# A product that begins half a row of retention earlier, and weight tiles that are converted later

## The chip, the cores and the metric

The kernel runs on one core of a Trainium2 chip. The metric is device time in microseconds for one launch. The version before took 604.58 us, the median of three runs (603.8, 604.58 and 605.14).

## The reference

Two stages follow each other. The first is a linear attention with decay (retention) over 4 batches, 8 heads, 768 tokens and a head width of 64:

```
state = gamma * state + k_t v_t^T
y_t   = scale * q_t state
```

Its output, laid out as 3072 tokens by 512 features, is x of a feed-forward layer with 2048 inner features:

```
h = x @ w_in                      # 3072x512 by 512x2048
g = h * clip(h + 3, 0, 6) / 6
out = g @ w_out                   # 3072x2048 by 2048x512
```

q, k and v are float32. Both weight matrices are float64 and are turned into float32 on the chip.

## The kernel before, in words

**Retention.** The 3072 tokens are 24 *rows* of 128 tokens. For a row, TensorE forms all scores of the eight heads (`sc`, L253, 16 matmuls), VectorE masks them (`am`, L301), TensorE forms the row's output from the state before it (`y`, L239, 8 matmuls) and from the masked scores (`y`, L259, 8 matmuls), and adds the row's keys and values to the running state (`uz`, L288, 8 matmuls), which ScalarE copies out (`state`, L297). VectorE scales the output (`xr`, L274), ScalarE writes its rounded high part and VectorE the remainder (`x`, L133 and L134). `burst(r)` does the scores of row r together with the output of row r-1; `sc` and `y` have one PSUM buffer each, so the scores of one row wait for the mask of the row before, and the output of one row for `xr` of the row before. The values are weighted per head by ScalarE for the first eight rows (`early`, L212, eight small instructions a row) and by GpSimd afterwards (L216).

**First product.** Four rows are a *unit* of 512 tokens, six units in all. `mm1(u, jj)` makes one 128x512 tile of h for unit u and feature tile jj (of 16): 12 matmuls, four blocks of the 512 features by three pairs of high and low parts. ScalarE adds 3 and takes the relu (L358), VectorE clips and multiplies (`g`, L359), and the tile goes out to a DRAM buffer (`gd`, L360). Three PSUM tiles and three SBUF tiles serve h and g.

**Weights of w_in.** Each of the 16 tiles of w_in is fetched as 512 KB of float64 (`st`, L104, two buffers, so the third fetch waits until the first has been converted) and converted by five VectorE instructions with one of ScalarE between them (L115 to L127), and then split into a high part (ScalarE, L133) and a low part (VectorE, L134). `build_w1(j)` is tile j. Tiles of w_out are converted in the same way (`build_w2`) during later units, with four more subtractions.

**Second product.** When all six units are through, `out` is made from `gd` by a seven-product scheme (L401 to L471). Nothing of it is touched here.

**Order.** TensorE's order is written by hand, in the order in which the program calls `burst` and `mm1`. VectorE, ScalarE, GpSimd and the transfer queue of SyncE are put in order by a scheduler when the program is built; on the chip each of them works its list off in that order. At the start `load` and `load_decay` of rows 0 to 7 are issued on SyncE, with four fetches of w_in between them (`WITH`, L51), and no transfer is issued before the one eight places ahead of it has landed. `attention` is a generator with one stop per row, `advance(n)` runs it up to its n-th stop, and the list `steps` (L366 to L369) says in which order the products are called: four of unit 0, then one of unit 0 and one of unit 1 in turn, then the other units.

Of the kernel before, what the change touches and what calls it, by code (L numbers as in the profile page):

```python
# [29 lines left out]
def retention_ffn(ctx: ExitStack, tc: tile.TileContext, qkv, w_in, w_out, dvs, dqs, out, B, H, S, D):  # L30
# [8 lines left out]
    NF = w_in.shape[0]  # L39
# [3 lines left out]
    NROW = NT // P  # L43
    ROWS_B = S // P
    UR = 4
# [2 lines left out]
    HM = DM // 2  # L48
    WARM = 14
    AHEAD = 2 * UR  # L50
    WITH = (0, 2, 3, 5)  # L51
    BUFS = {"lkt": 1, "lqt": 2, "lvn": 2, "lkn": 1}
    SPARE = ("lkn", "lkt", "lqt", "lqt")
    BLK = 2 * P
# [47 lines left out]
    def fetch(src):  # L102
        st = wst.tile([P, src.shape[-1]], I64, tag="st", name=nm("st"), bufs=2)
        nc.sync.dma_start(out=st, in_=src)  # L104
        return st
# [26 lines left out]
    def split(hi, lo, src):  # L132
        nc.scalar.activation(out=hi, in_=src, func=AF.Copy)  # L133
        nc.vector.tensor_tensor(out=lo, in0=src, in1=hi, op=ALU.subtract)  # L134
# [8 lines left out]
    def w1_block(j, k):  # L143
        s, o = divmod(j * NK + k, 14)
        if s not in w1s:
            w1s[s] = place([P, 14, 2, P], F32R, nm("w1"), s == 0)
        return w1s[s], o

    def build_w1(j, st=None):
        w = to_f32(fetch(w_in[j]) if st is None else st).rearrange("p (k n) -> p k n", k=NK)  # L150
        k = 0
        while k < NK:
            t, o = w1_block(j, k)
            n = min(NK - k, 14 - o)
            split(t[:, o : o + n, 0], t[:, o : o + n, 1], w[:, k : k + n])
            k += n
# [31 lines left out]
    def load(r):  # L188

        t = rows[r] = {}
        if r < AHEAD and r % 2 == 0:
            early[r] = wpool.tile([P, 7, NPAIR, P], F32, tag="w", name=nm("early"), bufs=NSLOT - 1)
        for i, (x, n) in enumerate((("kt", 1), ("qt", 0), ("vn", 3), ("kn", 2))):
            o = r % 2 * 4 + i
            if r < AHEAD and o < 7:
                t[x] = early[r // 2 * 2][:, o]
            else:  # L200
                tag = SPARE[r // 2] if r < AHEAD else f"l{x}"
                t[x] = apool.tile([P, NPAIR, P], F32, tag=tag, name=nm(x), bufs=BUFS[tag])
            if x != "kn" or r % ROWS_B < ROWS_B - 1:
                nc.sync.dma_start(out=t[x].rearrange("p h n -> p (h n)"), in_=qkv[r, n])
        if r >= AHEAD:
            decay(r)
# [13 lines left out]
    def load_decay(r):  # L220
        if r < AHEAD:
            if "dq" not in early:
                early["dq"] = wpool.tile([P, ROWS_B, NPAIR, P], F32, tag="w", name=nm("early"), bufs=NSLOT - 1)
            t = early["dq"][:, r % ROWS_B]
        else:
            t = apool.tile([P, NPAIR, P], F32, tag="dq", name=nm("dq"), bufs=1)
        rows[r]["dq"] = t
        if r < ROWS_B or r >= AHEAD:
            nc.sync.dma_start(out=t.rearrange("p h n -> p (h n)"), in_=dqs[r % ROWS_B])
# [82 lines left out]
    def attention():  # L312

        st = []
        for r in range(AHEAD):
            load(r)
            load_decay(r)
            if r in WITH:
                st.append(fetch(w_in[len(st)]))
        decay(0)  # L320
        for r in range(NROW + 1):
            if r == AHEAD:
                burst(r, new=False)
                yield
                burst(r, old=False)
            else:
                burst(r)
            if st and r in (0, 2, 3, 4):
                build_w1(len(WITH) - len(st), st.pop(0))
            if r + 1 < AHEAD:  # L330
                decay(r + 1)
            if r >= AHEAD - 1 and r + 1 < NROW:
                load(r + 1)
            if AHEAD <= r < NROW:
                load_decay(r)
            yield

    gen = attention()
    done = 0

    def advance(n):

        nonlocal done
        while done < min(n, NROW + 2):
            next(gen)
            done += 1

# [15 lines left out]
    order = ExitStack()  # L363
    order.enter_context(tc.manual_schedule(engines={mybir.EngineType.PE}))

    steps = [(0, jj) for jj in range(UR)]  # L366
    for jj in range(NF):
        steps += [(0, jj + UR)] * (jj + UR < NF) + [(1, jj)]
    steps += [(u, jj) for u in range(2, NU) for jj in range(NF)]  # L369
    advance(UR + 1)  # L370
    n_w1, n_w2 = len(WITH), 0
    for n, (u, jj) in enumerate(steps):
        if (u, jj) == (NU - 1, 0):
            att.close()
            late = ctx.enter_context(tc.tile_pool(name="late", bufs=1, side="right", reuse_waits="tile"))
        while n_w1 < min(NF, jj + 4):
            build_w1(n_w1)
            n_w1 += 1
        if jj in WHEN.get(u, ()):
            build_w2(n_w2)  # L380
            n_w2 += 1
        end = mm1(u, jj)
        if n < UR:
            advance(UR + 2 + n)
        elif u == 1:
            advance(2 * UR + 2 + int((jj + 1) / NF * UR + 0.5))
        elif 1 < u < NU - 1:
            advance(UR * (u + 1) + 2 + int((jj + 1) / NF * UR + 0.5))
    order.close()
    ph1.close()  # L390

# [146 lines left out]
```

## Time and profile before

| what | value |
|---|---|
| median of three runs | 604.58 us |
| the profiled execution's own time | 606.66 us |
| its span, first to last instruction | 604.9 us |
| TensorE (PE) busy | 588.3 us, 97% of the span |
| VectorE (DVE) busy | 457.4 us, 76% |
| ScalarE (ACT) busy | 253.1 us, 42% |
| GpSimd (POOL) busy | 18.0 us, 3% |
| mean granted clock of TensorE | 0.991 |

A page of the profile shows one execution. The share of busy time is a mean over stages with different limits, and a TensorE that runs at half its clock counts as busy. So the stretches of the first 140 us are read one by one: which engine has idle time in them, what ended it, and which clock was granted.

### The profile page before, as it was taken

To read this page: it belongs to the slowest core of one execution; us is meant where nothing else is said; L and a number is where in the kernel's file an instruction comes from. 1 tells how busy PE (TensorE), PEld (TensorE's weight loads), DVE (VectorE), ACT (ScalarE), POOL (GpSimd) and SP (SyncE) were. 2 spreads that over 40 slices of the span, in tenths; PEclk is the share of its full clock that TensorE was granted. 3 is DMA by queue.
4 is the path that set the end of the run, shared out by engine and by line. 5 is a ranking of instruction groups with operands and counts; after the bars stand their busy time and mean duration, and the time that the engine had idled before them with its cause. 6 is when DMAs were issued, how large, how long until landed. Compare 5 with 4: busy or idle time off the path is not lost.

```text
span 604.9 us, 12611 instructions
## 1 busy us (share of the span) xinstructions
PE 588.3 (97%) x4988; PEld 524.5 (87%) x4988; DVE 457.4 (76%) x960; ACT 253.1 (42%) x540; POOL 18.0 (3%) x24
## 2 busy tenths in 40 slices
PE   7688999999999999999999999999999999999997
PEld 6567788777888888888888889999999999999997
DVE  4779999999433597334336969998899889988983
ACT  5663554445222343222225545444444444444441
POOL 0001000000100000000000000000000000000000
PEclk9879999999999999999999999999999999999999
DMA  8965777665754457444334435443444344434411
GB/s 325 390 226 172 226 260 246 207 235 185 257 170 166 163 206 265 151 173 172 136 125 153 159 117 178 140 141 105 140 140 141 105 140 140 142 113 135 143 64 36
DMA packets 64731, 104.13 MB, mean 172 GB/s; under 512 B 5792, under 2 KB 30880, under 8 KB 64672
## 3 DMA queue, kind: packets, MB, share of 16 engines
q1 hardware_dynamic: 64528, 103.31, 50.7%
q8 instruction: 39, 0.64, 0.5%
q14 instruction: 20, 0.16, 0.1%
q10 hardware_dynamic: 144, 0.02, 0.0%
HBM read 71.85 MB, written 31.46 MB: 171 GB/s over the span
## 4 chain that ended last, share of the span: by engine, by line
PE 78%; DVE 14%; DMA 3%; issue 2%; SPq 1%; ACT 0%; DVEq 0%; ACTq 0%
PE o L440 40%; PE h L354 32%; PE y L259 3%; PE sc L253 2%; DVE g L359 2%; DMA st<-in_w_in 2%; DVE wb L121 2%; DVE w L134 2%; DVE am L301 2%; DVE we L124 2%; DVE ww L127 1%; PE y L239 1%; DMA early<-in_qkv 1%; DVE xr L274 1%; DVE ws L86 1%
## 5 line engine op out<-in xcount | busy, mean ns | idle before, releaser
L354 PE MATMUL h<-x,w 128*128 128x512 f32 x1152 | 272.4, 395 | 4.2 <-ACT x L133 2.2
L354 PEld LDWEIGHTS h<-x,w 128*128 128x128 f32 x1152 | 215.5, 189 | 53.6 <-DVE g L359 2.8
L440 PEld LDWEIGHTS o<-w,gc 128*128 128x128 f32 x2016 | 239.9, 191 | 0.1
L440 PE MATMUL o<-w,gc 128*128 128x256 f32 x2016 | 239.9, 282 | 0.0
L359 DVE SCALAR_TENSOR_TENSOR g<-g,h 128x512 f32<-128x512 f32 x96 | 65.7, 685 | 86.0 <-ACT g L358 85.7
L358 ACT ACTIVATE g<-h,three 128x512 f32<-128x512 f32 x96 | 65.5, 684 | 100.0 <-PE h L354 92.9
L133 ACT ACTIVATE gc<-gr 128x256 fp32r<-128x256 f32 x144 | 49.6, 408 | 117.8 <-PE o L440 114.1
L134 DVE TENSOR_TENSOR gc<-gr,gc 128x256 fp32r<-128x256 f32 x144 | 52.7, 420 | 20.1 <-ACT gc L133 20.1
L134 DVE TENSOR_TENSOR gc<-gsum,gc 128x768 fp32r<-128x768 f32 x96 | 62.0, 687 | 5.6 <-ACT gc L133 5.6
L133 ACT ACTIVATE gc<-gsum 128x768 fp32r<-128x768 f32 x96 | 54.7, 618 | 0.1
L133 ACT ACTIVATE w<-ww 128x384 fp32r<-128x384 f32 (+2 forms) x34 | 18.8, 556 | 50.9 <-DVE ww L127 48.4
L301 DVE TENSOR_TENSOR am<-sc,mask 128x1024 f32<-128x1024 f32 x24 | 29.2, 1216 | 0.0
L119 ACT ACTIVATE we<-we,ebias 128x512 int32<-128x512 int32 x32 | 22.9, 715 | 11.7 <-DVE we L115 11.5
L216 POOL TENSOR_TENSOR vn<-vn,cst_sb 128x512 f32<-128x512 f32 x16 | 17.2, 1078 | 272.0 <-DMA vn<-in_qkv 272.0
L124 DVE SCALAR_TENSOR_TENSOR we<-st,we 128x512 int32<-128x512 int32 x32 | 22.7, 711 | 0.0
L134 DVE TENSOR_TENSOR w<-ww,w 128x384 fp32r<-128x384 f32 (+2 forms) x34 | 20.3, 601 | 3.1 <-ACT w L133 2.9
L127 DVE SCALAR_TENSOR_TENSOR ww<-wb,we 128x512 f32<-128x512 f32 x32 | 22.1, 690 | 0.7
L121 DVE SCALAR_TENSOR_TENSOR wb<-st,wb 128x512 f32<-128x512 uint32 x32 | 22.0, 686 | 0.2
L89 DVE TENSOR_TENSOR gsum<-gr 128x256 f32<-128x256 f32 x48 | 20.4, 425 | 2.0 <-DMA gr<-gd 0.6
L133 ACT ACTIVATE x<-xr 128x512 fp32r<-128x512 f32 x24 | 15.1, 629 | 14.3 <-DVE xr L274 14.3
L86 DVE TENSOR_TENSOR gsum<-gr,gsum 128x256 f32<-128x256 f32 x48 | 20.2, 421 | 0.8
L115 DVE TENSOR_SCALAR we<-st 128x512 int32<-128x512 int32 x32 | 13.5, 422 | 9.2 <-DMA st<-in_w_in 8.9
(50 smaller groups left out, 349.8 us busy)
## 6 DMA issues: line engine op xcount, KB each, us to landing
gd<-g SPq DMA_DIRECT2D x96, 256.0 KB, 2.5
gr<-gd SPq DMA_DIRECT2D x96, 256.0 KB, 3.2
st<-in_w_in SPq DMA_DIRECT2D x16, 512.0 KB, 4.3
st<-in_w_out SPq DMA_DIRECT2D x16, 512.0 KB, 3.9
early<-in_qkv SPq DMA_DIRECT2D x28, 256.0 KB, 6.0
out<-ot SPq DMA_DIRECT2D x11, 512.0 KB, 2.8
kn<-in_qkv SPq DMA_DIRECT2D x16, 256.0 KB, 4.4
kt<-in_qkv SPq DMA_DIRECT2D x16, 256.0 KB, 3.9
```

Of the source, the lines that this page charges most:

```text
L86: return nc.vector.tensor_tensor(out=out_, in0=a, in1=b, op=ALU.subtract)
L119: nc.scalar.activation(out=e, in_=e, func=AF.Relu, scale=8.0, bias=ebias)
L121: nc.vector.scalar_tensor_tensor(out=y, in0=lo.bitcast(U32), scalar=2.0**-32, in1=b, op0=ALU.mult, op1=ALU.add)
L124: nc.vector.scalar_tensor_tensor(out=e, in0=hi, scalar=-2147483648, in1=e, op0=ALU.bitwise_and, op1=ALU.bitwise_or)
L127: nc.vector.scalar_tensor_tensor(out=w, in0=y, scalar=2.0**-20, in1=e.bitcast(F32), op0=ALU.mult, op1=ALU.mult)
L133: nc.scalar.activation(out=hi, in_=src, func=AF.Copy)
L134: nc.vector.tensor_tensor(out=lo, in0=src, in1=hi, op=ALU.subtract)
L301: nc.vector.tensor_tensor(out=new["am"].rearrange("p h a n -> p (h a) n"), in0=sc.rearrange("p h a n -> p (h a) n"), in1=mask[:, None, :]. ...
L354: nc.tensor.matmul(h, t[:, o, a], xs[u][b][:, k], start=k + n == 0, stop=(k, n) == (NK - 1, 2), skip_group_check=True)
L358: nc.scalar.activation(out=g, in_=h, func=AF.Relu, bias=three)
L359: ins = nc.vector.scalar_tensor_tensor(out=g, in0=g, scalar=6.0, in1=h, op0=ALU.min, op1=ALU.mult)
L440: nc.tensor.matmul(ps, gc[:, a, LEFT[i], jj, :], wc[:, RIGHT[i], b_], start=first and j == 0 and n == 0, stop=j == NFP - 1 and n == 2, ski ...
```

## The change

Five things are altered, all at the start of the program:

- The four early fetches of w_in stand behind rows 0, 3, 4 and 6 of the loads instead of rows 0, 2, 3 and 5.
- The burst of row 4 is cut in two, as that of row 8 was before: first the output of row 3, then a stop, then the scores of row 4.
- Tiles 1, 2 and 3 of w_in are converted behind the first half of row 4, behind its second half and behind row 5, instead of behind rows 2, 3 and 4.
- The number of products of unit 0 ahead of the first one of unit 1 goes from five to six (`LEAD`), and the rows that come one behind each product are rows 4 (second half) to 8 (first half).
- The counts given to `advance` are one higher, since there is one stop more.

```diff
-    WITH = (0, 2, 3, 5)
+    WITH = (0, 3, 4, 6)
+    LEAD = UR + 1
...
-            if r == AHEAD:
+            if r in (UR, AHEAD):
                 burst(r, new=False)
+                if r == UR:
+                    build_w1(1, st[1])
                 yield
                 burst(r, old=False)
             else:
                 burst(r)
-            if st and r in (0, 2, 3, 4):
-                build_w1(len(WITH) - len(st), st.pop(0))
+            if r == 0:
+                build_w1(0, st[0])
+            elif r in (UR, UR + 1):
+                build_w1(r - 2, st[r - 2])
...
-        while done < min(n, NROW + 2):
+        while done < min(n, NROW + 3):
...
-    steps = [(0, jj) for jj in range(UR)]
+    steps = [(0, jj) for jj in range(LEAD)]
     for jj in range(NF):
-        steps += [(0, jj + UR)] * (jj + UR < NF) + [(1, jj)]
+        steps += [(0, jj + LEAD)] * (jj + LEAD < NF) + [(1, jj)]
...
-        if n < UR:
+        if n < LEAD:
             advance(UR + 2 + n)
         elif u == 1:
-            advance(2 * UR + 2 + int((jj + 1) / NF * UR + 0.5))
+            advance(2 * UR + 3 + int((jj + 1) / NF * UR + 0.5))
         elif 1 < u < NU - 1:
-            advance(UR * (u + 1) + 2 + int((jj + 1) / NF * UR + 0.5))
+            advance(UR * (u + 1) + 3 + int((jj + 1) / NF * UR + 0.5))
```

How the engines' lists move is shown at three places. The names carry a number that tells buffers apart; the lines of the changed kernel are one to five higher.

TensorE around the first four products, before (`h_493`, `h_572`, `h_660` and `h_741` are the products of unit 0 with tiles 0 to 3; each `sc` is the scores of a row, from row 4 on):

```order
L253 MATMUL sc_430<-early_152 64x128 x16
L259 MATMUL y_421<-am_400,early_136 64x128 x8
L288 MATMUL uz<-early_152 64x64 x8
L354 MATMUL h_493<-x_258,w_19_221 128x512 x12
L239 MATMUL y_510<-early_152,state_398 64x128 x8
L253 MATMUL sc_519<-early_152 64x128 x16
L259 MATMUL y_510<-am_469,early_152 64x128 x8
L354 MATMUL h_572<-x_258,w_19_221 128x512 x12
```

And in the changed kernel (`h_431` and `h_510` are the products with tiles 0 and 1):

```order
L240 MATMUL y_399<-early_136,state_329 64x128 x8
L260 MATMUL y_399<-am_389,early_136 64x128 x8
L359 MATMUL h_431<-x_258,w_19_221 128x512 x12
L254 MATMUL sc_448<-early_150 64x128 x16
L289 MATMUL uz<-early_150 64x64 x8
L359 MATMUL h_510<-x_258,w_19_221 128x512 x12
L240 MATMUL y_527<-early_150,state_387 64x128 x8
L254 MATMUL sc_536<-early_150 64x128 x16
```

The scores and the state of row 4 have moved from ahead of the first product to behind it, and the second product comes ahead of the output of row 4.

VectorE from the second row on, before (`xr_317` is the output of row 1, `we_334` the second tile of w_in):

```order
L134 TENSOR_TENSOR x_258<-xr_259,x_258 128x4x128
L115 TENSOR_SCALAR we_334<-st_142 128x512
L116 TENSOR_SCALAR wb_333<-st_142 128x512
L121 SCALAR_TENSOR_TENSOR wb_333<-st_142,wb_333 128x512
L274 TENSOR_TENSOR xr_317<-y_283,early_126 128x512
L301 TENSOR_TENSOR am_331<-sc_292,mask 128x1024
```

And in the changed kernel (`xr_317` and `xr_375` are the outputs of rows 1 and 2, `we_421` the second tile of w_in):

```order
L135 TENSOR_TENSOR x_258<-xr_259,x_258 128x4x128
L275 TENSOR_TENSOR xr_317<-y_283,early_126 128x512
L302 TENSOR_TENSOR am_331<-sc_292,mask 128x1024
L135 TENSOR_TENSOR x_258<-xr_317,x_258 128x4x128
L116 TENSOR_SCALAR we_421<-st_148 128x512
L117 TENSOR_SCALAR wb_420<-st_148 128x512
L122 SCALAR_TENSOR_TENSOR wb_420<-st_148,wb_420 128x512
L125 SCALAR_TENSOR_TENSOR we_421<-st_148,we_421 128x512
L275 TENSOR_TENSOR xr_375<-y_341,early_126 128x512
```

The first instruction of the second tile stood ahead of the output of row 1 and stands now ahead of the output of row 2.

VectorE around the first products' results, before (`g_506` and `g_585` are the results of the first two products, `ww_473` the fourth tile of w_in, `we_562` the fifth):

```order
L127 SCALAR_TENSOR_TENSOR ww_473<-wb_471,we_472 128x512
L134 TENSOR_TENSOR w_19_221<-ww_473,w_19_221 128x2x128
L134 TENSOR_TENSOR w_50_482<-ww_473,w_50_482 128x2x128
L359 SCALAR_TENSOR_TENSOR g_506<-g_506,h_493 128x512
L274 TENSOR_TENSOR xr_545<-y_510,early_126 128x512
L301 TENSOR_TENSOR am_549<-sc_519,mask 128x1024
L134 TENSOR_TENSOR x_544<-xr_545,x_544 128x4x128
L115 TENSOR_SCALAR we_562<-st_559 128x512
```

And in the changed kernel (`g_444` and `g_523` are the first two results, `ww_479` the third tile of w_in, `we_499` the fifth; the fourth, `we_569` from `st_168`, stands nine rows after `we_499`):

```order
L128 SCALAR_TENSOR_TENSOR ww_479<-wb_477,we_478 128x512
L135 TENSOR_TENSOR w_19_221<-ww_479,w_19_221 128x4x128
L364 SCALAR_TENSOR_TENSOR g_444<-g_444,h_431 128x512
L302 TENSOR_TENSOR am_475<-sc_448,mask 128x1024
L364 SCALAR_TENSOR_TENSOR g_523<-g_523,h_510 128x512
L116 TENSOR_SCALAR we_499<-st_496 128x512
L117 TENSOR_SCALAR wb_498<-st_496 128x512
L275 TENSOR_TENSOR xr_562<-y_527,early_126 128x512
```

Before, four tiles of w_in are converted ahead of the first result; now three are, both first results stand ahead of the fifth tile, and the fourth tile is converted behind the fifth.

## Rows read from the trace of the kernel before

**Rows 1.** Busy time of each engine by stretch: from and to in us, the stretch's length, then for PE, PEld, DVE, ACT and POOL busy us and instructions, then the granted clock of TensorE (1.00 is 2.4 GHz, 0.50 is 1.2 GHz), the DMA share and GB/s.

```profile
17.50:21.00 3.50, 0.76 (x20) 0.52 (x24) 3.34 (x6) 2.24 (x6) 0.00 (x0) 1.00 1.06 398
21.00:24.50 3.50, 3.50 (x50) 3.17 (x52) 2.86 (x5) 2.54 (x8) 0.00 (x0) 0.51 1.04 383
...
29.00:31.00 2.00, 0.17 (x6) 0.03 (x2) 1.91 (x4) 1.58 (x5) 0.00 (x0) 1.00 1.06 389
31.00:38.00 7.00, 6.13 (x20) 4.10 (x24) 4.93 (x9) 4.25 (x15) 0.00 (x0) 0.52 0.49 186
38.00:49.00 11.00, 11.00 (x168) 9.01 (x160) 9.18 (x15) 6.80 (x20) 1.24 (x1) 1.00 0.76 253
49.00:50.50 1.50, 0.49 (x10) 0.30 (x13) 1.50 (x2) 1.21 (x2) 0.00 (x0) 1.00 0.68 251
...
62.50:100.00 37.50, 37.50 (x334) 30.81 (x334) 37.12 (x67) 18.28 (x32) 1.04 (x1) 1.00 0.72 241
100.00:130.00 30.00, 29.94 (x192) 23.86 (x189) 29.76 (x64) 13.96 (x24) 1.05 (x1) 1.00 0.67 225
130.00:140.00 10.00, 9.17 (x40) 6.90 (x39) 9.94 (x18) 4.46 (x8) 1.06 (x1) 1.00 0.53 177
140.00:200.00 60.00, 60.00 (x536) 49.43 (x538) 29.08 (x50) 18.34 (x31) 4.18 (x4) 1.00 0.59 197
200.00:600.00 400.00, 400.00 (x3216) 371.58 (x3209) 302.49 (x686) 161.49 (x346) 7.45 (x7) 1.00 0.43 143
```

**Rows 2.** The chain of waits, in order of time: start and length in us, then what the end of the program hung on in that time.

```profile
10.24 7.36 DMA st<-in_w_in
17.63 0.43 DVE we L115
...
137.03 0.69 DVE g L359
137.76 5.76 PE h L354 x24
```

**Rows 3.** The timeline of TensorE: start us, length us, engine, line, operation, tiles, shapes, count, and in brackets the idle time before and what ended it.

```profile
15.93 1.09 PE L259 MATMUL y<-am,early 128*64 128x128 f32 x16
...
19.77 0.67 PE L239 MATMUL y<-early,state 64*64 64x128 f32 x16 [2.28 <-DVE xr L274]
...
31.13 0.69 PE L354 MATMUL h<-x,w 128*128 128x512 f32 x1 [1.96 <-ACT x L133]
32.56 5.06 PE L354 MATMUL h<-x,w 128*128 128x512 f32 x11 [0.74 <-DVE x L134]
...
45.62 0.64 PE L288 MATMUL uz<-early 128*64 128x64 f32 x16
46.19 3.03 PE L354 MATMUL h<-x,w 128*128 128x512 f32 x12
...
52.75 3.02 PE L354 MATMUL h<-x,w 128*128 128x512 f32 x12
...
62.30 2.80 PE L354 MATMUL h<-x,w 128*128 128x512 f32 x11 [0.37 <-DVE x L134]
65.03 1.10 PE L253 MATMUL sc<-qt,kt 64*64 64x128 f32 x32
66.07 0.69 PE L288 MATMUL uz<-vn,kn 128*64 128x64 f32 x16
66.68 5.74 PE L354 MATMUL h<-x,w 128*128 128x512 f32 x24
```

**Rows 4.** The timeline of VectorE, with the same columns.

```profile
19.03 0.68 DVE L274 TENSOR_TENSOR xr<-y,early 128x512 f32<-128x512 f32 x1
...
38.38 0.69 DVE L359 SCALAR_TENSOR_TENSOR g<-g,h 128x512 f32<-128x512 f32 x1 [1.90 <-ACT g L358]
...
51.25 1.53 DVE L124 SCALAR_TENSOR_TENSOR we<-st,we 128x512 int32<-128x512 int32 x1
...
54.35 0.42 DVE L116 TENSOR_SCALAR wb<-st 128x512 int32<-128x512 int32 x1
54.69 0.69 DVE L134 TENSOR_TENSOR w<-ww,w 128x512 fp32r<-128x512 f32 x1
55.29 0.69 DVE L274 TENSOR_TENSOR xr<-y,early 128x512 f32<-128x512 f32 x1
55.89 1.22 DVE L301 TENSOR_TENSOR am<-sc,mask 128x1024 f32<-128x1024 f32 x1
57.02 0.68 DVE L134 TENSOR_TENSOR x<-xr,x 128x512 fp32r<-128x512 f32 x1
```

**Rows 5.** The timeline of ScalarE, with the same columns: the eight weightings of one row's values, and the first relu.

```profile
20.29 2.00 ACT L212 ACTIVATE early<-early,cst_sb 128x64 f32<-128x64 f32 x8
...
37.66 0.69 ACT L358 ACTIVATE g<-h,three 128x512 f32<-128x512 f32 x1 [1.67 <-PE h L354]
```

**Rows 6.** Transfers that SyncE issued: the third and the fifth fetch of w_in in the queue's timeline (issued at).

```profile
14.37 0.33 SPq L104 DMA_DIRECT2D st<-in_w_in  x1
...
30.40 0.33 SPq L104 DMA_DIRECT2D st<-in_w_in  x1
```

**Rows 7.** The view of transfers, asked for the moments of these two issues: size of one and us from issue to landing.

```profile
st<-in_w_in SPq DMA_DIRECT2D x1, 512.0 KB, 7.9
...
st<-in_w_in SPq DMA_DIRECT2D x1, 512.0 KB, 5.8
```

## The prediction

> **What bounds the kernel now.** First the stretches: TensorE has no idle time from 140 us to 600 us at a granted clock of 1.00, and 0.06 and 0.83 us between 100 and 140 us [rows 1]. So an edit at the start is worth what it moves the point from which TensorE runs without a break. The chain of waits says what sets that point: the end hangs on VectorE up to 137.03 us and on TensorE from 137.76 us [rows 2]. The timeline of TensorE then shows the early waits: 2.28 us for the output of row 1, which stood on VectorE behind the first instruction of w_in's second tile, and that waited for its transfer until 17.63 us [rows 2, 3]; 1.96 and 0.74 us before the first product, for x of row 3. TensorE also loses time that isn't idle: after the wait that ends at 19.77 us the granted clock falls to about 0.5 for 21 to 24.5 us, and after the one that ends at 31.13 us again, up to 38 us [rows 1, 3]. That is the level of 1.2 GHz; eleven matmuls take 5.06 us there and 2.80 us at 2.4 GHz [rows 3].
>
> VectorE is in order: it stood 1.90 us until 38.38 us for the first product's result [rows 4], while the fifth tile of w_in, issued at 30.40 us, had landed 5.8 us later, at 36.2 us [rows 6, 7]. So where VectorE's list holds a result of a product, VectorE waits for that product whatever else is ready.
>
> I compare at one point: the start of the first product behind (1,0), the products (0,0) to (0,5) and the scores and state of row 8. Before, that is the second product of the pair that starts at 66.68 us, so 66.68 + 5.74/2 = 69.5 us [rows 3]. What TensorE has to do behind it is the same in both kernels.
>
> **The change part by part.** No instruction is added or removed; waits are moved. I walk the new order with these prices: on VectorE, start to start, 0.34 us for L115 and L116, 0.60 for an instruction of 512 columns, 1.13 for a mask [rows 4], hence 3.1 us for a tile of w_in (2 x 0.34 + 4 x 0.60) and 2.3 for a row. On TensorE 2.8 us for a product at 2.4 GHz and 0.45 a matmul at 1.2 GHz (5.06/11), 1.0 for scores, 0.6 for a state, 0.9 for the masked output [rows 3]. The relu is 0.7 [rows 5].
>
> *Fetches.* The second tile of w_in takes the place of the third before, less one tile: that was issued at 14.37 us and landed 7.9 us later, at 22.3 us [rows 6, 7]; a 512 KB tile less at some 390 GB/s [rows 1] is 1.3 us, so it lands at about 20.9 us. The values of row 3 land by the same reckoning at about 18.3 us.
>
> *Rows 1 to 3.* The output of row 1 ends at 17.0 us (15.93 + 1.09) [rows 3], and VectorE takes it at once instead of at 19.03 us [rows 4]. The mask of row 2 is done at 18.8 us. ScalarE's list now has three of row 3's weightings (0.25 us each [rows 5]) ahead of x of row 1, so x is done at 20.7 us. Then VectorE waits for the second tile until 20.9 us, with the output of row 2 behind it, and works on it to 23.0 us: the wait that stood ahead of row 1 stands ahead of row 2. TensorE, idle from 21.8 us, waits for that output until 23.7 us and 0.6 us more for the mask of row 3. That is as long as the wait that ended at 19.77 us, after which the clock fell, so I take 1.2 GHz from here: the output of row 3 ends at 27.1 us, its x at 29.2 us.
>
> *First product.* It starts at 28.5 us, not 31.13 us, and runs steadily from 29.3 us, not 32.56 us. At 1.2 GHz it ends at 34.7 us, before at 37.6 us. The gain so far is 3 us.
>
> *Results and later tiles.* VectorE has finished the third tile at 32.9 us, and the next in its list is the first result. It stands until the product's end and the relu have passed, 35.5 us: 2.6 us. The mask of row 4 follows, to 37.3 us. Next is the second result: its product starts at 36.2 us behind the scores and state of row 4, ends at 39.1 us, and the result can start at 39.9 us: 2.6 us more. Nothing hides these 5.2 us; the fourth tile, which landed near 32.3 us, stands behind them. Before, the same stretch held one such wait of 1.90 us and four tiles were already done.
>
> *Fourth product.* Its tile is finished only behind the fifth tile, the third result, the outputs of rows 4 and 5 and the masks of rows 5 and 6. From 39.9 us that is 0.6 for the second result, 3.1 for the fifth tile, 0.6 for the third result, two outputs with one x between them (1.8), two masks (2.3), and 2.8 of the fourth tile (two 0.34, three 0.60, half a split), 11.2 us, and 0.5 us for handovers and for the output of row 4: 51.6 us. The third product ran from 41.4 to 44.2 us, the output of row 5 waits 1.1 us for a mask, and TensorE is free at 48.5 us. It starts two matmuls at 50.6 us and the rest at 51.6 us: about 2.7 us of waiting that wasn't there, and the lead over the old start at 52.75 us [rows 3] is down to 1.1 us.
>
> *Up to the second unit.* A wait of that length was followed by 1.2 GHz both times before, one of about 1 us at 49.2 us was not [rows 1], so I take most of this product at 1.2 GHz; it ends at 55.6 us. The fifth product and the output of row 7 bring TensorE to 63.0 us, the sixth to 65.8 us. VectorE needs until 68.1 us for x of row 7: from 51.6 us it has the rest of a split, two tiles and most of a third, three results, two rows' work and one wait of 1.5 us for the fourth result. So (1,0) starts in earnest at 68.1 us, before at 62.30 us [rows 3], with one product more behind it (2.8 us). After this wait again 1.2 GHz for most of it: it ends at 72.5 us, and with scores and state of row 8 (1.6 us) the point is reached at 74.1 us.
>
> **Sum.** 74.1 - 69.5 = 4.6 us later. Against it stand the 0.89 us that TensorE waited between 100 and 140 us [rows 1]: a TensorE that comes later finds VectorE done. Net 3.7 us. The profiled execution, 606.66 us (its span of 604.9 us and 1.8 us around it), would become 610.4 us; the median of the runs lies 2.1 us lower, at 604.58 us, and I put the difference on that: 608.3 us.
>
> Costs that no row shows. The fetch of the fifth tile stands on SyncE behind the store of the first result, so it is issued near 36.7 us; with 3.7 us as of an idle queue, landing is at 40.4 us, just in time, and with the 5.8 us of rows 7 at 42.5 us, up to 2.0 us on VectorE's path. I take nothing, since most transfers of the start are through by then. VectorE had one instruction of 1.53 us where its kind takes 0.69 [rows 4], and I don't know whether such come again; the sum has none, and one or two would add 0.8 to 1.7 us. The moved counts of `advance` and the reads of the list of fetches cost nothing, since they are done when the program is built.
>
> The clock carries much of the sum. A rule of the Trainium skill speaks against my use of it: the page "TensorE: Matmul & The Clock Gate", section "HAM oscillation — how this bites in real kernels", warns of idle gaps longer than any wait named here, so by it none of these waits would bring the clock down. The trace disagrees: the clock fell after waits of 2.28 and 1.96 us [rows 1, 3]. By that rule the time would be that of the first rival.
>
> **Rivals.** *The clock stays up (faster).* Walked with 2.4 GHz throughout, the output of row 3 ends at 26.0 us, the first product at 31.1 us, the first result at 32 us and the second at 36.2 us, the waits of VectorE shrink to 0.5 and 0.7 us, (1,0) starts at 62.9 us and the point comes at 67.1 us, 2.4 us earlier than before; with the 0.89 us gone that is 601.3 us. It decides at the two waits near 22 and 24 us: if they are short or fall so that the clock holds, the early start is kept. For it: one wait of 1 us left the clock up [rows 1]. Against it: the one of the same length didn't.
>
> *The clock falls only once, up to the first product.* Then the fourth product and (1,0) run at 2.4 GHz and the point comes at 70.8 us, 1.3 us later, net 0.4 us: 605.0 us. For it: the waits near 49 and 67 us stand between stretches of long matmuls. Against it: the one at 31.13 us was followed by these too.
>
> *Slower still.* The fifth tile lands late or VectorE has its long instructions again: 1.7 us more, 610.0 us.
>
> That the change doesn't do what it says I leave out: in the new lists the first product does stand ahead of row 4's scores.
>
> **How the numbers follow.** My forecast has a chance of 0.57 with a range of its own from 606.0 to 610.5 us; the clock that stays up 0.12; one fall 0.17; slower still 0.14. What a measurement of this kernel can tell from no change is 0.2%, 1.2 us, so the same is 603.4 to 605.8 us. The one fall is the same in two thirds of its cases (0.11) and slower in the rest (0.06); the clock that stays up is faster. So faster 0.12, same 0.11, slower 0.77. The range, 603.5 to 611.5 us, leaves out the first rival and the end of the last one.
>
> **What would show it.** First matmul of a product near 28.5 us; waits of VectorE for the first two results, each over 1.5 us; a wait of TensorE for the fourth tile near 49 to 51 us and for x of row 7 near 66 to 68 us; granted clock near 0.5 behind these; no wait of TensorE from 75 to 200 us. The prediction is wrong if VectorE's waits for the results are under 1 us, or if the point I compare at comes before 70 us.

## The result and the profile after

The changed kernel takes 608.89 us, the median of eight runs (606.51 to 610.69); the kernel before, on the same chip, 604.78 us. The ratio is 1.0062, with a 95% interval from 1.0041 to 1.0082: slower by 4.1 us. The profiled execution took 610.69 us, with a span of 609.0 us.

The chain of waits, in order of time (start us, length us, what the end hung on):

```profile
42.21 1.14 DVE am L302
45.16 1.33 DVE wb L122
46.49 1.45 DVE we L125
49.65 5.67 PE h L359 x12
67.76 4.03 PE h L359 x11
```

Where the chain before ran over the transfer of w_in's second tile [rows 2], it now runs over transfers for the rows up to 25.5 us and then, between 42 and 72 us, over VectorE and two slow products. TensorE's timeline, with the columns of [rows 3]:

```profile
24.55 0.67 PE L240 MATMUL y<-early,state 64*64 64x128 f32 x16 [0.61 <-DVE xr L275]
28.23 0.50 PE L359 MATMUL h<-x,w 128*128 128x512 f32 x1 [1.46 <-ACT x L134]
29.10 2.83 PE L359 MATMUL h<-x,w 128*128 128x512 f32 x11 [0.37 <-DVE x L135]
...
49.65 5.65 PE L359 MATMUL h<-x,w 128*128 128x512 f32 x12 [3.65 <-ACT w L134]
...
66.95 0.50 PE L359 MATMUL h<-x,w 128*128 128x512 f32 x1 [1.30 <-ACT x L134]
67.76 4.02 PE L359 MATMUL h<-x,w 128*128 128x512 f32 x11 [0.30 <-DVE x L135]
...
73.68 5.73 PE L359 MATMUL h<-x,w 128*128 128x512 f32 x24
...
141.02 3.02 PE L359 MATMUL h<-x,w 128*128 128x512 f32 x12 [0.71 <-DVE g L364]
144.20 3.01 PE L359 MATMUL h<-x,w 128*128 128x512 f32 x12 [0.16 <-DVE g L364]
147.14 0.67 PE L240 MATMUL y<-qt,state 64*64 64x128 f32 x16
147.63 0.51 PE L254 MATMUL sc<-qt,kt 64*64 64x128 f32 x12
```

The first product runs steadily 3.5 us earlier than before (29.10 us, before 32.56 us), and at 2.4 GHz besides: eleven matmuls in 2.83 us. That lead is gone behind the fourth product. It waits 3.65 us for its tile of w_in and then runs at half clock, 5.65 us instead of 3.0 us; with it and the scores, output and state of row 7, which stand behind it now and stood ahead of it before, TensorE is through at 57.9 us, before at 55.8 us. The point of comparison, the product behind (1,0), comes at 73.68 us; before it came at 69.5 us. The scores of row 12, which stand behind the last of the early waits, begin at 147.63 us. In the kernel before they stand at

```profile
143.94 0.51 PE L253 MATMUL sc<-qt,kt 64*64 64x128 f32 x12
```

so the two executions are 3.69 us apart there. Behind it neither waits in the first stage: row 23 begins at 301.13 us and at 297.44 us, again 3.69 us.

VectorE's timeline, with the columns of [rows 4]:

```profile
19.47 0.69 DVE L275 TENSOR_TENSOR xr<-y,early 128x512 f32<-128x512 f32 x1 [1.63 <-PE y L260]
21.80 0.42 DVE L116 TENSOR_SCALAR we<-st 128x512 int32<-128x512 int32 x1
...
32.01 0.69 DVE L135 TENSOR_TENSOR w<-ww,w 128x512 fp32r<-128x512 f32 x1 [0.70 <-ACT w L134]
32.69 0.69 DVE L364 SCALAR_TENSOR_TENSOR g<-g,h 128x512 f32<-128x512 f32 x1
33.30 1.22 DVE L302 TENSOR_TENSOR am<-sc,mask 128x1024 f32<-128x1024 f32 x1
37.33 0.69 DVE L364 SCALAR_TENSOR_TENSOR g<-g,h 128x512 f32<-128x512 f32 x1 [2.82 <-ACT g L363]
37.93 0.42 DVE L116 TENSOR_SCALAR we<-st 128x512 int32<-128x512 int32 x1
...
43.90 0.42 DVE L116 TENSOR_SCALAR we<-st 128x512 int32<-128x512 int32 x1
...
45.16 1.33 DVE L122 SCALAR_TENSOR_TENSOR wb<-st,wb 128x512 f32<-128x512 uint32 x1
46.42 1.52 DVE L125 SCALAR_TENSOR_TENSOR we<-st,we 128x512 int32<-128x512 int32 x1
```

VectorE stands 2.82 us for the second product's result. What it takes at 37.93 us is the fifth tile; the fourth, which had been fetched long before, follows it at 43.90 us. That tile is what the fourth product waits for. How much VectorE stands in all is one row of the view by stretch, up to the result that ends the wait of 0.71 us at 141.02 us (length, DVE busy and instructions, granted clock, DMA share, GB/s):

```profile
8.20:140.30 132.10, 120.04 (x216) 0.95 0.72 246
```

In the kernel before, up to the result that ended the wait there, at 137.03 us [rows 2]:

```profile
8.20:137.00 128.80, 120.80 (x214) 0.96 0.73 252
```

VectorE's idle time in the start is 132.10 - 120.04 = 12.06 us, before 128.80 - 120.80 = 8.0 us: 4.06 us more. Of these, 1.25 us lie ahead of the first tile, which VectorE took at 9.49 us here and at 8.24 us before; its fetch stands at the same place in both programs, and in the other runs of the changed order it was taken between 8.25 and 9.13 us, so that part varies with the execution. The granted clock, by stretch as in [rows 1]:

```profile
31.00:38.00 7.00, 7.00 (x115) 5.32 (x113) 3.49 (x6) 5.12 (x17) 0.00 (x0) 1.00 0.80 278
38.00:49.00 11.00, 7.20 (x112) 5.71 (x108) 10.58 (x17) 5.19 (x13) 2.29 (x2) 0.98 0.69 243
49.00:50.50 1.50, 0.85 (x2) 0.50 (x2) 1.50 (x3) 0.90 (x3) 0.00 (x0) 0.50 0.86 276
...
69.50:73.00 3.50, 3.50 (x38) 2.45 (x36) 2.39 (x5) 1.19 (x3) 0.00 (x0) 0.58 0.45 132
```

It held through the first product, where the kernel before had 0.52, and fell at the fourth product and at (1,0). It had fallen once before that in this execution, in the first rows, behind a wait of 2.75 us that ended with the late first tile (granted clock 0.58 from 11 to 15 us):

```profile
11.10 1.98 PE L254 MATMUL sc<-early 64*64 64x128 f32 x32 [2.75 <-DVE am L302]
```

### The profile page after: what moved, and what is told of

Its sections match the earlier page's. It is cut to its first block, busy times and chain, and to the rows that moved or that the text cites. A ratio compares the mean times of both kernels' runs of the same rounds, so it can differ in the third digit from the quotient of the medians.

```text
span 609.0 us, 12600 instructions
## 1 busy us (share of the span) xinstructions
PE 588.8 (97%) x4988; PEld 524.3 (86%) x4988; DVE 456.9 (75%) x960; ACT 254.1 (42%) x540; POOL 18.4 (3%) x24
## 4 chain that ended last, share of the span: by engine, by line
PE 79%; DVE 14%; DMA 4%; issue 2%; ACT 1%; SPq 0%; DVEq 0%; ACTq 0%
PE o L445 39%; PE h L359 33%; PE y L260 2%; DVE g L364 2%; PE sc L254 2%; DVE wb L122 2%; DMA early<-in_qkv 2%; DVE w L135 2%; DMA early<-in_decays_y 2%; DVE we L125 1%; DVE ww L128 1%; PE y L240 1%; DVE am L302 1%; PE uz L289 1%; DVE we L116 1%
## 5 line engine op out<-in xcount | busy, mean ns | idle before, releaser
L302 DVE TENSOR_TENSOR am<-sc,mask 128x1024 f32<-128x1024 f32 x24 | 29.2, 1216 | 0.0
L90 DVE TENSOR_TENSOR gsum<-gr 128x256 f32<-128x256 f32 x48 | 20.4, 425 | 2.0 <-DMA gr<-gd 0.5
L87 DVE TENSOR_TENSOR gsum<-gr 128x256 f32<-128x256 f32 x48 | 20.1, 418 | 0.0
```

The lines of the kernel that those rows point to most:

```text
L87: return nc.vector.tensor_tensor(out=out_, in0=a, in1=b, op=ALU.subtract)
L302: nc.vector.tensor_tensor(out=new["am"].rearrange("p h a n -> p (h a) n"), in0=sc.rearrange("p h a n -> p (h a) n"), in1=mask[:, None, :]. ...
```

## The experiments

Each has been timed in five rounds against the kernel before on the same chip. "Row 12" is the start of row 12's scores in the profiled execution; there the kernel before has 143.94 us and the changed one 147.63 us. The profiled execution of before took 2.1 us more than its median, so its rows show where time goes, and the medians how much.

**Which tile comes first.** The program calls for the fifth tile ahead of the second product and for the fourth only behind row 5. The first run turns these two round and leaves all else as changed:

```diff
-        while n_w1 < min(NF, jj + 4):
+        while n_w1 < min(NF, jj + 4 - (n == 1)):
```

> The changed kernel, with the fifth tile of w_in converted one product later, so that the fourth stands ahead of it on VectorE and fills the wait for the second result. Theory 'order of the conversions': TensorE's wait of 3.65 us for the fourth tile falls under 1 us, the half clock behind it goes too, and the time comes down by 3 to 5.5 us, to 603.5 to 606 us (0.998 to 1.002 of before). Theory 'the clock': the waits of the first rows bring it down wherever the tiles stand; within 1.5 us of the changed kernel, 607.5 to 610 us. Theory 'the sixth product': x of row 7 still comes late; 1 to 2 us come back, 607 us.

Measured 605.0 us, a ratio of 0.9999 (0.9981 to 1.0017): the whole loss is gone. Its TensorE timeline:

```profile
46.74 3.03 PE L359 MATMUL h<-x,w 128*128 128x512 f32 x12
52.40 1.41 PE L254 MATMUL sc<-early 64*64 64x128 f32 x32 [2.62 <-issue]
...
137.64 5.73 PE L359 MATMUL h<-x,w 128*128 128x512 f32 x24 [0.63 <-DVE g L364]
```

The fourth product starts without a wait, at 46.74 us. But the kernel isn't faster than before either, although its first product starts at 28.80 us: 2.62 us are lost ahead of the scores of row 7, which need the mask of row 6 (VectorE works on it from 51.08 us), and 0.63 us at 137 us, about as in the kernel before (0.68 us).

The reverse is the kernel before with the fourth tile converted behind row 6, so behind the fifth:

```diff
-            if st and r in (0, 2, 3, 4):
+            if st and r in (0, 2, 3, 6):
```

> The kernel before with one thing of the change: the fourth tile of w_in is converted behind row 6, and so behind the fifth tile, while TensorE uses it before. Theory 'order of the conversions': that alone brings the loss, 3 to 5 us slower than before, 607.5 to 610 us, with a wait of TensorE of 2 us or more ahead of the fourth product. Any theory that needs the early product or the sixth one: 604 to 606 us.

Measured 611.34 us, 1.0104 (1.0086 to 1.0121), more than the change itself.

```profile
38.06 0.69 DVE L359 SCALAR_TENSOR_TENSOR g<-g,h 128x512 f32<-128x512 f32 x1 [5.19 <-ACT g L358]
...
52.10 1.10 PE L253 MATMUL sc<-early 64*64 64x128 f32 x32 [3.44 <-issue]
...
55.51 3.26 PE L354 MATMUL h<-x,w 128*128 128x512 f32 x12 [0.81 <-ACT w L133]
...
66.25 4.10 PE L354 MATMUL h<-x,w 128*128 128x512 f32 x11 [0.31 <-DVE x L134]
```

VectorE stands 5.19 us for the first result, before 1.90 us [rows 4]: the fourth tile no longer fills that time. TensorE's waits stand at the same two places, around the fourth product (3.44 and 0.81 us) and at (1,0), where part of the product again runs at half clock (4.10 us). So putting the fourth tile behind the fifth is enough to bring a loss, without an early first product. The expectation had the wait at the product itself; most of it lies one step ahead, at the scores. That the loss is larger than the change's has a reason of its own in part: here the fifth tile is fetched from 39.15 us on, and VectorE stands another 1.64 us for it until 44.01 us, which it doesn't in the changed kernel.

**The other parts of the change, one by one.** Put into the kernel before, six products of unit 0 instead of five ahead of the first of unit 1:

```diff
+    LEAD = UR + 1
-    steps = [(0, jj) for jj in range(UR)]
+    steps = [(0, jj) for jj in range(LEAD)]
-        steps += [(0, jj + UR)] * (jj + UR < NF) + [(1, jj)]
+        steps += [(0, jj + LEAD)] * (jj + LEAD < NF) + [(1, jj)]
```

> The kernel before with six products of unit 0 ahead of the first one of unit 1 and nothing else. Theory 'the sixth product': most of the loss is here, 607 to 609 us (1.004 to 1.007 of before). Theory 'order of the conversions': under 2.5 us slower, since all of the first four tiles are still converted ahead of the first result; 604.5 to 607 us. Theory 'the clock': no difference, 604 to 605.5 us.

Put into the kernel before, later fetches, with the conversions one row later where their data comes later:

```diff
-    WITH = (0, 2, 3, 5)
+    WITH = (0, 3, 4, 6)
-            if st and r in (0, 2, 3, 4):
+            if st and r in (0, 3, 4, 5):
```

> The kernel before with the early fetches of w_in behind rows 0, 3, 4 and 6 and the conversions behind rows 0, 3, 4 and 5; row 4 in one piece and five products ahead. Theory 'order of the conversions': the tiles still come in the order of their use, so within 1 us of before, 604 to 605.8 us. Theory 'later tiles cost by themselves': 606.5 us or more.

The early first product, that is the changed kernel with fetches and conversions as before:

```diff
-    WITH = (0, 3, 4, 6)
+    WITH = (0, 2, 3, 5)
-                if r == UR:
-                    build_w1(1, st[1])
...
-            if r == 0:
-                build_w1(0, st[0])
-            elif r in (UR, UR + 1):
-                build_w1(r - 2, st[r - 2])
+            if st and r in (0, 2, 3, 4):
+                build_w1(len(WITH) - len(st), st.pop(0))
```

> The changed kernel with the fetches and conversions of before: row 4 in two pieces and six products, tiles behind rows 0, 2, 3 and 4. Theory 'order of the conversions': the fourth tile is ahead of the second result and of the fifth tile, so most of the loss goes: 605 to 607 us, no wait of TensorE over 1.5 us for a tile. Theory 'the sixth product' or 'row 4 in two pieces': it stays at 608 to 610 us.

Measured 605.5 us (ratio 1.0001, 0.9985 to 1.0016), 605.09 us (1.0006, 0.9991 to 1.002) and 604.53 us (1.0, 0.9987 to 1.0012): none can be told from before. So neither part does harm by itself, and an early product (29.41 us in the last of the three) gains nothing by itself.

**Is it the clock?** Matmuls of no use fill the two waits, so that TensorE doesn't stand there:

```diff
+        fill = {(0, 3): 13, (1, 0): 5}.get((u, jj), 0)
+        for n in range(fill):
+            t, o = w1_block(0, 0)
+            nc.tensor.matmul(h, t[:, o, 0], xs[0][0][:, 0], start=True, stop=True, skip_group_check=True)
```

> The changed kernel with idle matmuls put into two waits of TensorE, 13 of 512 columns ahead of the fourth product and 5 ahead of the first one of unit 1 (their results are overwritten). Nothing else waits less, only the clock has no reason to fall there. Theory 'the clock': the fourth product takes 3 instead of 5.65 us, and the time comes down by 2.5 to 4 us, to 605 to 606.5 us. Theory 'order of the conversions': VectorE's waits for the first results and the wait for the tile stay, and 0.5 to 2.5 us come back through the fourth result: 606.5 to 608.5 us.

Measured 609.99 us, 1.0075 (1.0056 to 1.0093): no faster than the changed kernel, though the granted clock is 1.00 from 38 to 200 us.

```profile
51.79 0.73 PE L363 MATMUL h<-x,w 128*128 128x512 f32 x2 [0.69 <-ACT w L134]
52.81 2.54 PE L363 MATMUL h<-x,w 128*128 128x512 f32 x10 [0.28 <-DVE w L135]
...
67.83 2.83 PE L363 MATMUL h<-x,w 128*128 128x512 f32 x11 [0.50 <-DVE x L135]
...
146.75 1.05 PE L254 MATMUL sc<-qt,kt 64*64 64x128 f32 x32
```

The fourth product is no longer slow, and (1,0) takes 2.83 us instead of 4.02; but the fourth product's tile is late as before, and (1,0) starts where it did in the changed kernel (67.83 and 67.76 us), since it waits for VectorE's x. By row 12 0.88 us of the 3.69 are regained in this execution, and none in the medians. One thing blurs it: here the first product ran partly at half clock (eleven matmuls in 3.98 us, behind the same waits of 1.46 and 0.37 us), and VectorE takes the second result at 39.27 us, 1.9 us later than in the changed kernel's profile. So the half clock behind these two waits isn't what the loss consists of; how much of it a clock held up might give back, under 1 us by this run, isn't settled.

**Is it GpSimd?** In the changed kernel the two long VectorE instructions lie beside GpSimd's weighting of rows 8 and 9:

```profile
44.91 1.04 POOL L217 TENSOR_TENSOR vn<-vn,cst_sb 128x512 f32<-128x512 f32 x1 [43.50 <-DMA vn<-in_qkv]
46.15 1.24 POOL L217 TENSOR_TENSOR vn<-vn,cst_sb 128x512 f32<-128x512 f32 x1 [0.20 <-DMA vn<-in_qkv]
```

ScalarE weights these rows instead, as it does the earlier ones:

```diff
-        if r < AHEAD:
+        if r < AHEAD + 2:
```

> The changed kernel with the values of rows 8 and 9 weighted by ScalarE instead of GpSimd. Two instructions of VectorE, 1.33 and 1.52 us long where their kinds take 0.68, lay beside GpSimd's two. Theory 'GpSimd holds VectorE up': both come back to 0.68 and the time is 0.7 to 2 us lower, 607 to 608.2 us. Theory 'something else, transfers for instance': they stay long, no difference.

Measured 610.51 us, 1.01 (1.0078 to 1.0121): no better.

```profile
47.21 0.83 ACT L213 ACTIVATE vn<-vn,cst_sb 128x64 f32<-128x64 f32 x3 [2.22 <-DMA vn<-in_qkv]
...
48.59 0.69 DVE L135 TENSOR_TENSOR w<-ww,w 128x512 fp32r<-128x512 f32 x1 [2.99 <-ACT w L134]
...
53.46 5.31 PE L359 MATMUL h<-x,w 128*128 128x512 f32 x12 [5.21 <-ACT w L134]
```

No VectorE instruction of 512 columns takes over 0.70 us around 45 us any more. But ScalarE, in order too, now stands 2.22 us for the transfer of the row's values, with the high part of the fifth tile behind it. VectorE stands 2.99 us for that, and the fourth tile comes behind it in VectorE's list, so the fourth product waits 5.21 us. Not all of that is ScalarE's: the first product ran at half clock in this execution, and VectorE took the second result at 39.59 us instead of 37.33 us, 2.26 us of the 3.81 us by which the fourth product starts later. This execution took 614.08 us, 3.6 us more than the median of its kernel; the median shows only that nothing was gained.

**Why does the early product gain nothing?** Once the tiles stand in the right order, TensorE still waits 0.6 to 1.1 us for a result near 133 to 138 us in each of the kernels of r1 to r4, and VectorE is busy for 39.6 to 39.7 of the 40 us from 100 to 140 us. A first attempt at that stretch converts w_out's tiles later:

```diff
-        while n_w1 < min(NF, jj + 4):
+        while n_w1 < min(NF, jj + 4 - (n == 1)):
...
-    WHEN = {1: (9, 12, 15), 2: (4, 8, 12), 3: (4, 12), 4: (4, 12), 5: (4, 6, 8, 10, 12, 14)}
+    WHEN = {2: (4, 8, 12), 3: (3, 6, 9, 12), 4: (4, 8, 12), 5: (4, 6, 8, 10, 12, 14)}
```

> The kernel of r1 with the three conversions of w_out in unit 1 moved to units 3 and 4. In all kernels so far TensorE waits 0.6 to 0.9 us for a result of VectorE near 135 to 141 us, so VectorE's work up to there may be what keeps an early product from paying. Theory 'VectorE sets the point near 137 us': that wait goes, and the time is 1 to 3 us lower, 602 to 604 us. Theory 'TensorE's early waits and clock set it': only the wait itself goes, 604.2 to 604.8 us.

Measured 605.09 us, 1.0008 (0.9994 to 1.0021). It tells nothing: between 70 and 135 us VectorE ran the same 20 subtractions for w_out's tiles as with the old table, since the scheduler had pulled the work forward again, and TensorE still waited 0.61 us at 135.31 us.

So VectorE is given less work: the fifth tile is left out, in the kernel before, in that of r1 and in that of r4. It is neither fetched nor converted, and its products read the fourth tile, so these three kernels leave out one of the 16 feature tiles; TensorE has the same number of matmuls.

```diff
     def build_w1(j, st=None):
+        if j == 4:
+            return
...
-            t, o = w1_block(jj, k)
+            t, o = w1_block(3 if jj == 4 else jj, k)
```

> The kernel before with the fifth tile of w_in (j = 4) neither fetched nor converted; its products use the fourth tile's numbers, so two of the 16 feature tiles of h are the same and one is left out. TensorE has the same matmuls, VectorE has 3.1 us less in the first 50 us. Theory (VectorE's list is what the whole start hangs on, up to the wait near 137 us): the waits of TensorE behind 40 us, which sum to some 2 us, go: 602.5 to 603.5 us. Rival (TensorE's own order sets the start): within 0.9 us of before, since that is all TensorE waits behind 100 us.

> The changed kernel with the fourth tile ahead of the fifth (as in r1), and the fifth tile left out in the same way. Theory (the first product starts 2 to 3 us earlier and VectorE's list hides that): with 3.1 us less on VectorE the wait of 2.6 us for row 6's mask and that of 0.6 us near 137 us go: 601 to 602 us, and 1 to 2 us below r9. Rival (the early start is worth nothing to TensorE, since it is given back as half clock): the same as r9 within 0.5 us.

> The early first product with the conversions of before (as in r4), and the fifth tile left out in the same way. Theory: as r10, 601 to 602 us. Rival: the same as r9 within 0.5 us.

Measured 604.91 us for the kernel before without the tile (1.0001, 0.9988 to 1.0013), 601.74 us for r1 without it (0.9945, 0.9927 to 0.9963) and 603.45 us for r4 without it (0.9967, 0.9953 to 0.9981). The same 3.1 us of VectorE's work are worth nothing in the old order, against the expectation, and 3.3 us in the new one. The stretch from 40 to 70 us, with the columns of [rows 1], first r9, then r10:

```profile
40.00:70.00 30.00, 27.79 (x313) 21.73 (x314) 27.84 (x45) 14.03 (x30) 2.30 (x2) 1.00 0.63 210
```

```profile
40.00:70.00 30.00, 28.90 (x310) 22.36 (x312) 29.78 (x49) 13.78 (x25) 2.37 (x2) 1.00 0.73 227
```

In r9 VectorE stands 30 - 27.84 = 2.16 us there, in the kernel before 0.61 us; the first product starts late, TensorE sets the pace, and the work taken away becomes idle time. In r10 VectorE stands 0.22 us, and the wait of 2.62 us ahead of row 7's scores is gone. The second wait that was to go didn't: TensorE waits 0.27 and 0.68 us at 131.94 and 135.65 us. r11 lies between, outside what either theory said. So the early start is real, and it is VectorE's list that takes it back: a product that starts 3 us earlier asks for masks, results and tiles 3 us earlier. The tile left out takes its fetch and ScalarE's part with it; that these counted isn't excluded by a run, but in r1 VectorE was busy for 29.20 of the 30 us and so hardly waited for either.

The last run takes no work away but puts some of it later: by the edit each tile from the fifth to the tenth is converted one product later than in the changed kernel (the expectation says fourth to eleventh; the fourth keeps its place and comes ahead of the fifth by that).

```diff
-        while n_w1 < min(NF, jj + 4):
+        while n_w1 < min(NF, jj + 4 - (1 <= n <= LEAD + 2)):
```

> The changed kernel, with each tile of w_in from the fourth to the eleventh converted one product later (three tiles ahead of the product instead of four), so that the fourth stands ahead of the fifth and fewer tiles stand ahead of the masks of rows 6 and 7. Nothing is left out. Theory (the early first product is worth its 2 to 3 us where VectorE's list has room for it): the mask of row 6 stands three instructions, 1.8 us, earlier in VectorE's list than in r1, the wait of 2.6 us ahead of its scores shrinks to 1 us, and part of it reaches the end: 602.5 to 604.5 us, 0.1 to 0.4% under before. Rival (VectorE gives it back by 137 us, since it has the same work up to there and is busy 39.7 of 40 us from 100 to 140): the same as before, 604.5 to 605.5 us, with a wait of 0.6 us or more near 137 us.

Measured 604.33 us, 0.9993 (0.9978 to 1.0009), as the rival had it.

```profile
64.64 5.74 PE L359 MATMUL h<-x,w 128*128 128x512 f32 x24
...
107.62 14.21 PE L359 MATMUL h<-x,w 128*128 128x512 f32 x60 [0.92 <-DVE g L364]
...
136.46 3.02 PE L359 MATMUL h<-x,w 128*128 128x512 f32 x12 [0.56 <-DVE g L364]
...
148.86 0.51 PE L359 MATMUL h<-x,w 128*128 128x512 f32 x1 [0.75 <-ACT x L134]
149.93 5.52 PE L359 MATMUL h<-x,w 128*128 128x512 f32 x23 [0.56 <-DVE x L135]
```

The early part works as meant: the point of comparison comes at 64.64 us, 4.9 us before the 69.5 us of the old order and nearly where r10 has it without the tile (64.17 us). Then 0.92, 0.56, 0.75 and 0.56 us are lost to VectorE, each where its list holds a tile's conversion ahead of a result or of a row's x. Set beside r10, which lacks the work, r12 is 0.5 us behind at the point of comparison, 0.8 us at row 12 (139.89 and 139.12 us) and 2.7 us at row 13 (155.38 and 152.72 us): the work put off in the first 60 us comes back by then. Against the profile of the kernel before, r12 still leads by 2.15 us at row 13 (157.53 us there); that profile lies 2.1 us above its own median, and in the medians no lead is left.

## Why the prediction was right, step by step

The time, the direction and the place of the loss came out: 608.89 us against 608.3, 3.69 us at row 12 against a net of 3.7. Not every step on the way did, and that the numbers meet so closely is in part luck: errors of up to 2.6 us cancelled.

*Fetches: not what set the pace in this execution.* VectorE took the second tile at 21.80 us without a wait. It had stood before that, 1.63 us, for the output of row 1 from TensorE, which ended at 19.4 us and not at 17.0: the first tile was late and the clock fell behind that wait. Whether the second tile landed near 20.9 us can't be read there.

*Rows 1 to 3: wrong on the way, right at the end by luck.* The waits of 1.9 and 0.6 us were 0.61 us and 0.47 us, and the clock stayed at 1.00 from 17.5 to 38 us. The x of row 3 came at 29.0 us all the same (29.2 forecast), since row 1 had come 2.4 us later than forecast and the waits behind it were shorter.

*First product: start right, clock wrong.* 28.23 and 29.10 us (28.5 and 29.3), but at 2.4 GHz; it ended at 31.9 us, not 34.7. (The price at half clock, 5.06/11, is 0.46 us a matmul and not 0.45; over a product that is 0.1 us.)

*Results and later tiles: the mechanism right, one of its two waits absent.* Of the two waits of 2.6 us the first wasn't there: with the product at 2.4 GHz, the result was ready before VectorE had finished the third tile, which cost 0.70 us for its high part. The second was 2.82 us. So 3.5 us in place of 5.2.

These four steps are those of one execution. In r7 the list of VectorE is the same up to the second result, and its profile follows the prediction: the output of row 1 ended at 17.0 us, the second tile was taken at 20.86 us behind a wait for its transfer (20.9 forecast), TensorE waited 2.11 and 0.42 us (1.9 and 0.6), and the first product ran at half clock, with both waits of VectorE behind it:

```profile
28.17 5.93 PE L359 MATMUL h<-x,w 128*128 128x512 f32 x12 [1.46 <-ACT x L134]
...
34.86 0.69 DVE L364 SCALAR_TENSOR_TENSOR g<-g,h 128x512 f32<-128x512 f32 x1 [2.21 <-ACT g L363]
...
39.59 0.69 DVE L364 SCALAR_TENSOR_TENSOR g<-g,h 128x512 f32<-128x512 f32 x1 [2.90 <-ACT g L363]
```

In seven profiles VectorE's list is the same up to the first result (the changed kernel, r1, r6, r7, r8, r10, r12). In five of them the first product ran at half clock for a part or the whole and VectorE then stood 1.14 to 2.21 us for the result; in two, the changed kernel's and r8's, the clock held and that wait was absent.

*Fourth product: right, with two errors that cancel.* It started at 49.65 us (50.6, and 51.6 for the rest), its wait 3.65 us (2.7). VectorE took the second result 2.6 us earlier than forecast (37.33 us, 39.9). Against that came the instructions of VectorE that are longer than their kind, which the sum had left out: 1.33 and 1.52 us where 0.69 is usual, 1.5 us together on the path to this tile. The fetch of the fifth tile, issued at 33.78 us, cost nothing: VectorE took it at 37.93 us without a wait. The 1.1 us that the prediction still counted as a lead over the old start at 52.75 us were none: the work on row 7 that stood ahead of this product before, 2.6 us of it, stands behind it now. The sum doesn't use that figure.

*Up to the second unit: right.* The fourth product at half clock ended at 55.3 us (55.6), (1,0) started at 67.76 us (68.1) and ended at 71.8 us (72.5); the point came at 73.68 us (74.1).

*Sum: right, with two terms off.* The loss to the point was 4.2 us (4.6). Of the 0.89 us that were to come back, the 0.83 us from 130 to 140 us did not: TensorE again waits 0.71 and 0.16 us near 141 and 144 us, before 0.16 and 0.68 us. The half microsecond that did come back, 4.2 - 3.69, lies elsewhere: from the scores of row 10 to those of row 11 the new kernel takes 25.05 us and the old 25.63 us, a stretch in which [rows 1] show hardly any idle time. The step failed in what it took for granted near 140 us: a later TensorE doesn't find VectorE done, because VectorE had stood for about the same time. That there is no wait from 75 to 200 us was wrong for the same reason.

Of the signs named, both waits of TensorE and the half clock behind them came; of VectorE's two waits over 1.5 us only the second came in this profile, and the prediction had named a wait under 1 us as a sign against it.

The clock decided less than its place in the working said. Half of the first rival's condition was met, the clock stayed up through the first product, and the kernel was still 4.1 us slower: VectorE's wait for the second result was 2.82 us, not the 0.7 us that the rival took for it. The rival's own times don't give 0.7: from the first result at 32 us, 0.6 for it and 1.1 for the mask leave 2.5 us up to 36.2. And with the clock held up at the two later waits (r6) it stayed slow. The trace bears out that the clock fell there, at waits of 3.65 us and of 1.30 and 0.30 us, and that it didn't fall at the first product behind 1.46 and 0.37 us; in r6 and r12 it was down for part of that product, behind the same two waits, so which waits do it isn't settled by these runs.

What is shown: the order of the fourth and fifth tiles in VectorE's list makes the loss (r1, r5), and VectorE's list hides the early start (r9, r10, r12; in r9 to r11 together with what else the tile takes). Left open: which of VectorE's conversions from 100 to 140 us could be put behind 140 us, since r8 didn't move them.

## What to carry to other kernels

Where an engine works its list off in order, read the list for the tile that is needed first, not for how many are ready: one tile behind another that is needed later cost 4 to 6 us here. An earlier start of one engine is worth something only if the engine that feeds it has idle time where the start moves its work; count that idle time up to the last wait before taking the lead into a sum. Taking a small piece of work off one engine can gain nothing (r7), where its new place makes another engine stand for a transfer with needed work behind it.

## What the hardware showed beside that

GpSimd's work holds up VectorE. The two weightings ended at 45.95 and 47.39 us; the VectorE instructions that had started meanwhile, at 45.16 and 46.42 us, ended at 46.49 and 47.94 us, 0.54 and 0.55 us later, and took 1.33 and 1.52 us instead of 0.69. With the weighting on ScalarE (r7) both were of usual length. Both VectorE instructions read two tiles in SBUF, the on-chip memory that holds the tiles. The Trainium skill, page "SBUF — State Buffer", section "Who interferes with whom", says that a VectorE instruction with two SBUF inputs contends with a GpSimd instruction that reads SBUF, by an exclusive lock on the ports that they share; the trace agrees. A GpSimd instruction of 1.04 to 1.24 us so cost VectorE 0.64 and 0.83 us.
